# One stay in the 64-row mode per step: moving the 64-row products of a fused FNet and MLP kernel

## Chip, core and metric

The kernel runs on one core of one Trainium2 chip. The metric is the device time of one execution in microseconds (us). Engine names are those of the profile: PE is TensorE's matmul, PEld its weight load, DVE is VectorE, ACT is ScalarE, POOL is GpSimd, SP is SyncE with the DMA queue. L290 is line 290 of the kernel.

## What is computed

The input x has 2048 tokens of 576 features. With xn the layer norm of x over the features, the result is

```
out = x + Re(DFT_seq(DFT_hidden(xn))) + relu(xn @ w1) @ w2
```

w1 is 576 x 4608 and w2 is 4608 x 576; the DFT matrices are inputs, and the real part is `Cr @ a - Ci @ b` of two hidden transforms a and b. Everything is float32 outside.

## The kernel before

**Number format.** Every float32 operand is scaled by a power of two and split into two float16 parts, a high one (index 0) and a low one (index 1). A product is then the sum of three float16 matmuls, high by high, high by low and low by high, accumulated in one PSUM bank. The 576 features are 4 blocks of 128 and a rest of 64.

**The first matrix of the MLP.** The hidden columns are worked through in 9 blocks b of 512 (FB), each in 4 f tiles i of 128 columns (NF). The tokens are worked through in 4 groups g of 512 (G). A step is one pair (b, g), 36 in all. For one f tile, `mlp1` opens a PSUM bank of the pool `ps1` (4 banks) and `mlp1_group` (L288 to L293) runs products of 128 x 512: the 12 of the four whole feature blocks, and one more, `(KM, 0, KM)`, which holds the rest twice over its 128 rows (high part of x in rows 0 to 63, low part in rows 64 to 127, against the high part of w1). What is still missing is the high part of x's rest against the low part of w1's rest, and that has only 64 rows. `mlp1_rest` (L300 to L306) runs it for a pair of f tiles with two 64-row products: the even f tile's on rows 0 to 63 and the odd one's on rows 64 to 127. For that, slot NKX of `xT` holds the high rest a second time in rows 64 to 127. Each of the two closes its f tile's bank.

**After a pair of f tiles**, `mlp1_out` (L308) reads the two banks: ACT L315 and L318 and DVE L319 to L323 form relu, its split and the sums that a seven-product (Strassen-Winograd) block multiplication needs, ACT L325 and DVE L326 split those sums. L323 is the last to read the odd bank, L320 among DVE's the last to read the high half of the even one.

**The second matrix.** `mlp2` (L330) runs one of the seven products q: 12 matmuls of 128 x 288 (L340) into a bank pair of the pool `ps2` (2 pairs), and DVE L346 adds the result to the accumulator.

**The order of a step** is written out in the loop at L642 to L679. The first matrix of step n runs beside the second matrix of step n-1: f tile 0, then q = 0 and 1; f tile 1, the 64-row pair, `mlp1_out` of pair 0, q = 2 and 3; f tile 2, then q = 4 and 5; f tile 3, the 64-row pair, `mlp1_out` of pair 1, q = 6. In between, `work()` takes pieces of the preparation of the next block's weights, and `passes` take the maxima of the sequence-DFT matrices. Steps 0 and 1 and half of step 2 (n == 2, with two f tiles made early) are written out ahead of the loop with other calls.

**What sets the order on an engine.** The framework's planner issues the instructions of each engine mostly in the order of the text; where by its own cost estimate an operand or a buffer isn't ready, it takes the next instruction that is. In the trace PE keeps the text's order in the steps from about 150 us on, and leaves it in the stretch before.

After the steps come the hidden DFT (L709) and the sequence DFT (L810), which the change doesn't touch.

Of the kernel before, what the change touches and what calls it, by code (L numbers as in the profile page):

```python
# [9 lines left out]
F32 = mybir.dt.float32  # L10
# [7 lines left out]
P = 128  # L18
# [6 lines left out]
NF = FB // P  # L25
NQ = NF // 2
G = 512
# [3 lines left out]
KT = 5  # L31
KM = 4
REM = D - KM * P
EH = D // 2
NKX = 2 * KM + 1
# [6 lines left out]
def kernel(  # L42
# [17 lines left out]
    nc = tc.nc  # L60
# [10 lines left out]
    ps1 = tc.alloc_tile_pool(name="ps1", bufs=4, space=PSUM)  # L71
# [96 lines left out]
    xT = [xpool[g].tile([P, NKX + 1, G], F16, name=f"xT{g}") for g in range(NG)]  # L168
# [6 lines left out]
    def stats(ts):  # L175

        n = len(ts)
        mv = small.tile([P, n, 2], F32, tag=f"mv{n}", name=f"mv{ts[0]}")
        sts = [small.tile([P, 2, 6], F32, tag="st", name=f"st{t}", bufs=4) for t in ts]
        for t, st in zip(ts, sts):  # L180
            for j in range(2):
                nc.vector.bn_stats(st[:, j, :], acc[t][:, j * EH : (j + 1) * EH])
                yield
        for i, st in enumerate(sts):
            nc.vector.bn_aggr(mv[:, i], st.rearrange("p a b -> p (a b)"))
            yield
        r0, u, r, sh = (
            small.tile([P, n], F32, tag=f"{a}{n}", name=f"{a}_{ts[0]}") for a in ("r0", "u", "r", "sh")
        )
        m, v = mv[:, :, 0], mv[:, :, 1]  # L190
        stt = nc.vector.scalar_tensor_tensor
        nc.scalar.activation(u, v, AF.Sqrt, bias=eps)
        nc.vector.reciprocal(r0, u)
        yield

        stt(u, v, EPS, r0, ALU.add, ALU.mult)
        yield
        nc.vector.tensor_tensor(u, u, r0, ALU.mult)
        yield
        nc.vector.tensor_scalar(u, u, -0.5 * SX, 1.5 * SX, ALU.mult, ALU.add)  # L200
        yield
        nc.vector.tensor_tensor(r, u, r0, ALU.mult)
        yield
        stt(sh, m, -1.0, r, ALU.mult, ALU.mult)
        for i, t in enumerate(ts):
            means[t], factors[t], shifts[t] = mv[:, i, 0:1], r[:, i : i + 1], sh[:, i : i + 1]

    def weave(steps, *others):

        others = list(others)  # L210
        for _ in steps:
            if others:
                others.pop(0)()
        for f in others:
            f()
# [3 lines left out]
    def normalize(t, eng=nc.vector):  # L219
        stage = dpool.tile([P, 5 * EH], F32, tag="d", name=f"xn{t}")  # L220
        xn = xns[t] = stage[:, :D]

        xs = xss[t] = stage[:, D : 2 * D].bitcast(F16)
        eng.tensor_scalar(xn, acc[t], means[t], factors[t], ALU.subtract, ALU.mult)  # L224
        nc.scalar.activation(xs[:, :D], acc[t], AF.Identity, bias=shifts[t], scale=factors[t])
# [56 lines left out]
    WK = [(kx, hl, k) for k in range(KM) for kx, hl in ((k, 1), (k, 0), (KM + 1 + k, 0))]  # L282
# [2 lines left out]
    WK0 = sorted(WK, key=lambda w: w[1])  # L285
    w1s, w2s, us, hs = {}, {}, {}, {}

    def mlp1_group(b, g, i, cols, ps, wk=WK):  # L288
        for n, (kx, hl, k) in enumerate(wk):
            nc.tensor.matmul(  # L290
                ps[:, cols], w1s[b, i // 2][:, hl, i % 2 * KT + k], xT[g][:, kx, cols],
                start=(n == 0), stop=(n == len(WK) - 1),
            )  # L293

    def mlp1(b, g, i, wk=WK):
        ps = ps1.tile([P, G], F32, tag="ps1", name=f"p1_{b}_{g}_{i}")
        mlp1_group(b, g, i, slice(0, G), ps, wk)
        return ps

    def mlp1_rest(b, g, i, *ps):  # L300

        for r, kx in enumerate((KM, NKX)):
            rows = slice(r * REM, (r + 1) * REM)
            nc.tensor.matmul(  # L304
                ps[r], w1s[b, i][rows, 1, r * KT + KM], xT[g][rows, kx], start=False, stop=True
            )  # L306

    def mlp1_out(b, g, i, pa, pb):  # L308

        h = hs[b, g, i] = mlp.tile([P, 2, 7, GH], F16, tag="h", name=f"h{b}_{g}_{i}", bufs=4)  # L310
        st = mlp.tile([P, 5, GH], F32, tag="stage", name=f"s{b}_{g}_{i}")
        stt = nc.vector.scalar_tensor_tensor
        a11, a21, a12, a22 = pa[:, :GH], pa[:, GH:], pb[:, :GH], pb[:, GH:]
        r21, s1, s2, s3, s4 = (st[:, n] for n in range(5))
        nc.scalar.activation(r21, a21, AF.Relu)  # L315
        for q, src in ((slice(A11, A11 + 1), a11), (slice(A12, A22 + 1), pb)):
            hi, lo = (h[:, n, q].rearrange("p a b -> p (a b)") for n in range(2))
            nc.scalar.activation(hi, src, AF.Relu)  # L318
            stt(lo, src, 0.0, hi, ALU.max, ALU.subtract)  # L319
        stt(s3, a11, 0.0, r21, ALU.max, ALU.subtract)  # L320
        stt(s1, a22, 0.0, r21, ALU.max, ALU.add)
        stt(s2, a22, 0.0, s3, ALU.max, ALU.subtract)
        stt(s4, a12, 0.0, s2, ALU.max, ALU.subtract)  # L323
        hi, lo = (h[:, n, S1 : S4 + 1] for n in range(2))
        order["s"] = nc.scalar.activation(hi, st[:, 1:], AF.Copy).ins  # L325
        order["lo"] = nc.vector.tensor_tensor(lo, st[:, 1:], hi, ALU.subtract).ins  # L326
# [121 lines left out]
    def prepare_block(b):  # L448

        wait = [lambda: None] * 2  # L450
        (m0, s0), (m1, s1) = prepare_w1(b, 0), prepare_w1(b, 1)
        return (
            [lambda: (load_w1(b, 0), load_w1(b, 1))] + wait
            + m0 + m1 + s0 + [lambda: load_w2(b, 0)] + s1 + [lambda: load_w2(b, 1)]
            + wait + prepare_w2(b)
        )
# [17 lines left out]
    ps = [ps1.tile([P, G], F32, tag="ps1", name=f"p1_0_0_{i}") for i in range(NF)]  # L474
# [78 lines left out]
    for t in (8, 9, 10, 11):  # L553
        N(t)
        E(t, GP)
    T(8)
    q2 = [mlp1(0, 1, 2)]
    T(9)
    q2.append(mlp1(0, 1, 3))
# [3 lines left out]
    early = [mlp1(0, 2, 0), mlp1(0, 2, 1)]  # L563
# [7 lines left out]
    def work():  # L571
        if todo:
            todo.pop(0)()
# [5 lines left out]
    def load_d(j):  # L579
        load_raw(("d", j), dft[:, :, j * EH : (j + 1) * EH], [P, KT, EH])  # L580

    def power_d(j):
        if j == 0:
            sc["d"], pw["d"], mx["d"] = cell("sd", 4), cell("pd", 4), cell("md", 4)
        m = slice(j, j + 1)
        magnitude(mx["d"][:, m], raws["d", j])
        power(sc["d"][:, m], pw["d"][:, m], mx["d"][:, m])
# [5 lines left out]
    def split_d(j):  # L593
        split(dsp[j][:, 0], dsp[j][:, 1], raws["d", j], sc["d"][:, j : j + 1])
# [47 lines left out]
    for n in range(2, len(steps)):  # L642
        b, g = steps[n]
        pb, pg = steps[n - 1]
        if g == 0 and b:
            if b + 1 < NB:
                todo += prepare_block(b + 1)
            else:
                todo += [lambda: (load_d(0), load_d(1)), lambda: None, new_d, lambda: None]
                for j in range(4):  # L650
                    todo += [lambda j=j: power_d(j), lambda j=j: split_d(j)]
                    if j < 2:
                        todo += [lambda j=j: load_d(j + 2), lambda: None]
                todo += [scales_d]
        if b == 0 and g + 1 < NG:
            with tc.issue_after(order["lo"]):
                weave(stats([(g + 1) * TG + i for i in range(TG)]))
        ps = []
        for i in range(NF):
            ps.append(early.pop(0) if n == 2 and i < 2 else mlp1(b, g, i, WK[:-1]))  # L660
            if i % 2:
                if n > 2 or i > 2:
                    mlp1_rest(b, g, i // 2, *ps[-2:])
                mlp1_out(b, g, i // 2, *ps[-2:])
            if b == 0 and g + 1 < NG:
                t = (g + 1) * TG + i
                normalize(t)
                remainder(t, nc.gpsimd)
                transposes(t)
            if n == 2 and i == 2:  # L670
                todo += prepare_block(1)
            for _ in range(1 if b else 3):
                work()
            for q in range(2 * i, min(2 * i + 2, 7)):
                mlp2(pb, pg, q)
            for _ in range(1 if b else 3):
                work()
            if n > 3 and i % 2 and passes:
                passes.pop(0)()  # L679
# [115 lines left out]
    for n, (p, kh) in enumerate(units):  # L795
# [4 lines left out]
        for i, (q, rq, first, row, col) in enumerate(PRODUCTS):  # L800
# [5 lines left out]
            ps, w = places[PLACE[i]], csp[m]  # L806
            for k in range(HK):
                r = R[kh * HK + k]
                for j, (a, c) in enumerate(((0, 0), (0, 1), (1, 0))):
                    nc.tensor.matmul(  # L810
                        ps, w[:, a, k], r[:, c, rq],
                        start=first and k == 0 and j == 0, stop=k == HK - 1 and j == 2,
# [4 lines left out]
            if kh and i in (2, 4, 5, 6):  # L817
                h, j = ((0, 0), (1, 1), (0, 1), (1, 0))[(2, 4, 5, 6).index(i)]
                rows = slice((p + h * NP) * P, (p + h * NP + 1) * P)
# [56 lines left out]
```

## Time and profile before

| | |
|---|---|
| three runs | median 1299.18 us, 1298.37 to 3428.88 |
| the profiled execution | 1299.04 us, span 1297.3 us |
| granted TensorE clock | 0.997 of full |
| PE busy | 1274.7 us, 98% of the span |
| DVE, ACT busy | 974.5 us (75%), 530.1 us (41%) |
| L290, 128x512 products | 1798 of 380 ns, 413.6 us |
| L340, 128x288 products | 3024 of 286 ns, 395.1 us |
| L304, 64x512 products | 134 of 386 ns, 26.1 us |

Durations of matmuls in the profile overlap: what one costs in a row of them is the distance between starts. The row's busy time is the union of its spans. "issue" as a releaser means that the engine waited for nothing that the profile shows.

### The profile page before, as it was taken

The numbers are of one execution on the slowest core, as the hardware profiler recorded it, in microseconds if no ns is written. First come the engines' busy times: TensorE is split into PE (matmuls) and PEld (weight loads), VectorE is DVE, ScalarE is ACT, GpSimd is POOL, SyncE is SP. The second block draws the span as 40 slices with busy tenths as digits, with TensorE's granted clock in tenths as the row PEclk, the third lists the DMA queues.
The fourth block names the chain that finished last, engine by engine and source line by source line (L and its number), as shares of the span: only waits on it lengthen the run. The fifth ranks groups of instructions, "written<-read, shape, count | busy, mean of one in ns | idle before, by whom it ended". The sixth has DMA issues, their size and how long they took to land.

```text
span 1297.3 us, 21890 instructions
## 1 busy us (share of the span) xinstructions
PE 1274.7 (98%) x9164; PEld 862.5 (66%) x9164; DVE 974.5 (75%) x1671; ACT 530.1 (41%) x794; POOL 33.8 (3%) x60
## 2 busy tenths in 40 slices
PE   8799999999999999999999999999999999999998
PEld 7565555565565655565555656677777777777777
DVE  8878878587596595685875985568678887888875
ACT  4834344343353442433433442234443333333332
POOL 2210000000000000000000000000000000000000
PEclk9999999999999999999999999999999999999999
DMA  6001213122122132131221222230024435243420
GB/s 240 32 11 59 73 48 127 49 85 91 49 90 83 45 99 67 50 126 50 73 103 50 86 88 86 104 136 17 1 70 158 142 115 165 97 147 121 140 84 19
DMA packets 38002, 112.75 MB, mean 87 GB/s; under 512 B 3984, under 2 KB 10640, under 8 KB 37904
## 3 DMA queue, kind: packets, MB, share of 16 engines
q1 hardware_dynamic: 37904, 111.36, 25.4%
q8 instruction: 71, 1.16, 0.4%
q14 instruction: 27, 0.22, 0.1%
HBM read 101.91 MB, written 9.44 MB: 86 GB/s over the span
## 4 chain that ended last, share of the span: by engine, by line
PE 87%; DVE 6%; DMA 2%; ACT 2%; issue 1%; SPq 1%; POOLq 0%; DVEq 0%; ACTq 0%
PE p L290 27%; PE p L340 26%; PE p L810 25%; PE pd L709 7%; PE p L304 2%; DVE acc L346 1%; DMA raw_d<-in_dft_dram 1%; DMA raw_w<-in_w_dram 1%; DVE w2s L165 1%; DVE h L319 0%; DMA f<-in_cre_dram 0%; ACT xT L247 0%; SPq L80 0%; DVE h L326 0%; DVE xn L224 0%
## 5 line engine op out<-in xcount | busy, mean ns | idle before, releaser
L290 PE MATMUL p<-xT,w1s 128*128 128x512 f16 (+1 forms) x2134 | 434.4, 355 | 2.0 <-ACT xT L247 1.7
L340 PE MATMUL p<-w2s,h 128*128 128x288 f16 x3024 | 395.1, 286 | 3.3 <-DVE acc L346 2.2
L340 PEld LDWEIGHTS <-h 128*128 128x128 f16 x3024 | 290.0, 98 | 104.2 <-issue 18.1
L810 PE MATMUL p<-R,cs 128*128 128x288 f16 x2688 | 329.4, 286 | 0.0
L290 PEld LDWEIGHTS <-w1s 128*128 128x128 f16 x2134 | 195.0, 98 | 189.6 <-issue 4.7
L810 PEld LDWEIGHTS <-cs 128*128 128x128 f16 x2688 | 263.0, 98 | 66.3
L346 DVE SCALAR_TENSOR_TENSOR acc<-p,c_ub,acc 128x576 f32<-128x576 f32 x252 | 204.2, 812 | 47.9 <-PE p L340 47.2
L164 ACT ACTIVATE cs<-c,sc_c 128x1024 f16<-128x1024 f32 x112 | 128.6, 1148 | 203.5 <-PE p L810 147.6
L165 DVE SCALAR_TENSOR_TENSOR cs<-c,sc_c,cs 128x1024 f16<-128x1024 f32 x112 | 143.6, 1282 | 50.1 <-ACT cs L164 41.8
L319 DVE SCALAR_TENSOR_TENSOR h<-p,h 128x256 f16<-128x256 f32 (+1 forms) x144 | 78.3, 551 | 120.7 <-ACT h L318 120.7
L325 ACT ACTIVATE h<-s 128x1024 f16<-128x1024 f32 x72 | 76.1, 1057 | 151.0 <-DVE s L323 151.0
L315 ACT ACTIVATE s<-p 128x256 f32<-128x256 f32 x72 | 27.5, 381 | 246.3 <-PE p L304 246.1
L709 PE MATMUL pd<-dsp,xT 128*128 128x288 f16 x896 | 110.2, 286 | 1.1 <-DVE acc L346 0.9
L326 DVE TENSOR_TENSOR h<-s,h 128x1024 f16<-128x1024 f32 x72 | 88.0, 1223 | 29.3 <-ACT h L325 28.9
L709 PEld LDWEIGHTS <-xT 128*128 128x128 f16 x896 | 87.7, 98 | 23.6 <-issue 1.4
L816 DVE SCALAR_TENSOR_TENSOR o<-p,us_c,o 128x288 f32<-128x288 f32 x112 | 57.4, 513 | 20.6 <-PE p L810 20.5
L635 ACT ACTIVATE f<-f 128x1024 f32<-128x1024 f32 x64 | 66.6, 1041 | 3.8 <-DMA f<-in_cre_dram 3.8
L318 ACT ACTIVATE h<-p 128x512 f16<-128x512 f32 (+1 forms) x144 | 62.8, 491 | 0.2 <-PE p L290 0.2
L164 ACT ACTIVATE w2s<-raw_w,c_sw 128x576 f16<-128x576 f32 (+1 forms) x54 | 43.1, 854 | 29.6 <-DVE raw_w L418 20.4
L165 DVE SCALAR_TENSOR_TENSOR w2s<-raw_w,c_sw,w2s 128x576 f16<-128x576 f32 (+1 forms) x54 | 48.1, 910 | 0.0
L164 ACT ACTIVATE w1s<-raw_w,c_sw 128x640 f16<-128x640 f32 x36 | 28.0, 826 | 17.5 <-DVE c_sw L107 17.4
L727 ACT ACTIVATE R<-pd,c_rho 128x288 f16<-128x288 f32 x48 | 23.8, 499 | 22.8 <-DVE T L721 13.1
(102 smaller groups left out, 676.4 us busy)
## 6 DMA issues: line engine op xcount, KB each, us to landing
f<-in_cre_dram SPq DMA_DIRECT2D x32, 512.0 KB, 3.6
f<-in_cim_dram SPq DMA_DIRECT2D x32, 512.0 KB, 3.5
c<-in_cre_dram SPq DMA_DIRECT2D x32, 512.0 KB, 4.3
c<-in_cim_dram SPq DMA_DIRECT2D x32, 512.0 KB, 4.7
raw_w<-in_w_dram SPq DMA_DIRECT2D x17, 640.0 KB, 4.1
raw_w<-in_w_dram SPq DMA_DIRECT2D x18, 576.0 KB, 3.8
acc<-in_x_dram SPq DMA_DIRECT2D x16, 288.0 KB, 6.0
spill<-acc SPq DMA_DIRECT2D x16, 288.0 KB, 2.5
```

What stands on the lines that cost most here:

```text
L164: nc.scalar.activation(hi, src, AF.Copy, scale=s)
L165: nc.vector.scalar_tensor_tensor(lo, src, s, hi, ALU.mult, ALU.subtract)
L290: nc.tensor.matmul(ps[:, cols], w1s[b, i // 2][:, hl, i % 2 * KT + k], xT[g][:, kx, cols], start=(n == 0), stop=(n == len(WK) - 1),)
L318: nc.scalar.activation(hi, src, AF.Relu)
L319: stt(lo, src, 0.0, hi, ALU.max, ALU.subtract)
L325: order["s"] = nc.scalar.activation(hi, st[:, 1:], AF.Copy).ins
L326: order["lo"] = nc.vector.tensor_tensor(lo, st[:, 1:], hi, ALU.subtract).ins
L340: nc.tensor.matmul(ps[:, c], h[:, x, qa, c * P : (c + 1) * P], w[:, y, qb], start=first and i == 0 and j == 0, stop=i == NQ - 1 and j == 2 ...
L346: nc.vector.scalar_tensor_tensor(o, ps, us[b], o, ALU.mult, ALU.add)
L635: nc.scalar.activation(f, f, AF.Abs, scale=2.0**-10, accum_out=sums_c[:, n, q : q + 1])
L709: nc.tensor.matmul(ps[j], xT[g][:, kx, c * P : (c + 1) * P], dsp[j][:, hl, k], start=(n == 0), stop=(n == len(XK) - 1),)
L810: nc.tensor.matmul(ps, w[:, a, k], r[:, c, rq], start=first and k == 0 and j == 0, stop=k == HK - 1 and j == 2, skip_group_check=not first,)
```

## The change

In each step from n = 3 on, all four 64-row products are issued at the head of f tile 1, behind f tile 0's 13 products and behind q = 0 and 1. The one of f tile 0 closes its bank; those of f tiles 1, 2 and 3 open theirs, so that from then on the four banks of `ps1` are held at once. The 13 products of f tiles 1, 2 and 3 then add to their banks and close them. Rows alternate as before: f tiles 0 and 2 on rows 0 to 63, f tiles 1 and 3 on rows 64 to 127. In step n = 2, f tiles 2 and 3 run a 14th product on 128 rows in place of the 64-row pair.

```diff
-    def mlp1_rest(b, g, i, *ps):
-        for r, kx in enumerate((KM, NKX)):
-            rows = slice(r * REM, (r + 1) * REM)
-            nc.tensor.matmul(
-                ps[r], w1s[b, i][rows, 1, r * KT + KM], xT[g][rows, kx], start=False, stop=True
-            )
+    def mlp1_step(b, g, i, ps):
+        if i == 1:
+            for j in range(NF):
+                r, kx = j % 2, (KM, NKX)[j % 2]
+                rows = slice(r * REM, (r + 1) * REM)
+                if j:
+                    ps.append(new_ps1(b, g, j))
+                nc.tensor.matmul(
+                    ps[j], w1s[b, j // 2][rows, 1, r * KT + KM], xT[g][rows, kx],
+                    start=(j > 0), stop=(j == 0),
+                )
+        if i == 0:
+            ps.append(new_ps1(b, g, 0))
+        mlp1_group(b, g, i, slice(0, G), ps[i], WK[:-1], start=(i == 0), stop=(i > 0))
...
         for i in range(NF):
-            ps.append(early.pop(0) if n == 2 and i < 2 else mlp1(b, g, i, WK[:-1]))
+            if n == 2:
+                ps.append(early.pop(0) if early else mlp1(b, g, i))
+            else:
+                mlp1_step(b, g, i, ps)
             if i % 2:
-                if n > 2 or i > 2:
-                    mlp1_rest(b, g, i // 2, *ps[-2:])
-                mlp1_out(b, g, i // 2, *ps[-2:])
+                mlp1_out(b, g, i // 2, *ps[i - 1 : i + 1])
```

`new_ps1` only opens a bank of `ps1`; `mlp1_group` takes `start` and `stop` so that a group can leave its bank open or add to an open one.

More of the change, by code (lines that the diff above doesn't have):

```diff
@@ L286, with mlp1_group @@
     w1s, w2s, us, hs = {}, {}, {}, {}
-    def mlp1_group(b, g, i, cols, ps, wk=WK):
+    def mlp1_group(b, g, i, cols, ps, wk=WK, start=True, stop=True):
         for n, (kx, hl, k) in enumerate(wk):
@@ L291, in mlp1_group, with new_ps1, mlp1 @@
                 ps[:, cols], w1s[b, i // 2][:, hl, i % 2 * KT + k], xT[g][:, kx, cols],
-                start=(n == 0), stop=(n == len(WK) - 1),
+                start=(start and n == 0), stop=(stop and n == len(wk) - 1),
             )
-    def mlp1(b, g, i, wk=WK):
-        ps = ps1.tile([P, G], F32, tag="ps1", name=f"p1_{b}_{g}_{i}")
-        mlp1_group(b, g, i, slice(0, G), ps, wk)
-        return ps
-    def mlp1_rest(b, g, i, *ps):
-        for r, kx in enumerate((KM, NKX)):
-            rows = slice(r * REM, (r + 1) * REM)
-            nc.tensor.matmul(
-                ps[r], w1s[b, i][rows, 1, r * KT + KM], xT[g][rows, kx], start=False, stop=True
-            )
+    def new_ps1(b, g, i):
+        return ps1.tile([P, G], F32, tag="ps1", name=f"p1_{b}_{g}_{i}")
+    def mlp1(b, g, i):
+        ps = new_ps1(b, g, i)
+        mlp1_group(b, g, i, slice(0, G), ps)
+        return ps
+    def mlp1_step(b, g, i, ps):
[12 more added lines that the diff above has]
+        mlp1_group(b, g, i, slice(0, G), ps[i], WK[:-1], start=(i == 0), stop=(i > 0))
     def mlp1_out(b, g, i, pa, pb):
```

## The prediction

> **What bounds the kernel now.** I read the page first, then the engines' busy time by stretch, then PE's timeline. The page's first part and its chain of waits say that PE is the bound and which lines carry it:
>
> ```profile
> PE 1274.7 (98%) x9164; PEld 862.5 (66%) x9164; DVE 974.5 (75%) x1671; ACT 530.1 (41%) x794; POOL 33.8 (3%) x60
> ...
> PE 87%; DVE 6%; DMA 2%; ACT 2%; issue 1%; SPq 1%; POOLq 0%; DVEq 0%; ACTq 0%
> PE p L290 27%; PE p L340 26%; PE p L810 25%; PE pd L709 7%; PE p L304 2%; DVE acc L346 1%; DMA raw_d<-in_dft_dram 1%; DMA raw_w<-in_w_dram 1%; DVE w2s L165 1%; DVE h L319 0%; DMA f<-in_cre_dram 0%; ACT xT L247 0%; SPq L80 0%; DVE h L326 0%; DVE xn L224 0%
> ```
>
> A share of busy time is a mean over stages, so the stage of the change is looked at by itself: three steps one after another (span, then busy us of PE, PEld, DVE, ACT, POOL).
>
> ```profile
> 591.33:613.70 22.37, 22.37 (x141) 13.34 (x140) 12.50 (x21) 6.49 (x12) 0.00 (x0) 1.00 0.15 48
> 613.70:636.07 22.37, 22.37 (x141) 13.34 (x140) 15.67 (x32) 10.69 (x18) 0.37 (x1) 1.00 0.15 48
> 636.07:658.44 22.37, 22.37 (x141) 13.32 (x140) 21.79 (x47) 10.68 (x18) 0.70 (x2) 1.00 0.31 106
> ```
>
> PE has no gap in any of them, and each takes 22.37 us to the hundredth. DVE has room in two and almost none in the third. So what PE is spared in a step shortens the step, as long as DVE keeps up. PE's timeline of one step (start, length, line, count) gives the prices:
>
> ```profile
> 591.65 0.39 PE L304 MATMUL p<-xT,w1s 64*128 64x512 f16 x2
> 591.97 1.65 PE L340 MATMUL p<-w2s,h 128*128 128x288 f16 x12
> 593.46 2.97 PE L290 MATMUL p<-xT,w1s 128*128 128x512 f16 x13
> 596.26 3.10 PE L340 MATMUL p<-w2s,h 128*128 128x288 f16 x24
> 599.20 2.97 PE L290 MATMUL p<-xT,w1s 128*128 128x512 f16 x13
> 602.10 0.39 PE L304 MATMUL p<-xT,w1s 64*128 64x512 f16 x2
> ```
>
> From starts to starts: 13 products of L290 take 2.80 us (593.46 to 596.26), 0.2155 each; 24 of L340 take 2.94 (596.26 to 599.20), 0.1225 each. The stays in the 64-row mode stand out under a finer timeline, where a weight load (PEld) is to be read beside the product that it is for:
>
> ```profile
> 613.71 0.38 PE L290 MATMUL p<-xT,w1s 128*128 128x512 f16 x1
> 614.02 0.10 PEld L304 LDWEIGHTS <-w1s 64*128 64x128 f16 x2 [0.42 <-issue]
> 614.02 0.39 PE L304 MATMUL p<-xT,w1s 64*128 64x512 f16 x2
> ...
> 614.34 0.10 PEld L340 LDWEIGHTS <-h 128*128 128x128 f16 x1 [0.23 <-issue]
> 614.34 0.30 PE L340 MATMUL p<-w2s,h 128*128 128x288 f16 x1
> ...
> 614.48 0.10 PEld L340 LDWEIGHTS <-h 128*128 128x128 f16 x1
> ```
>
> The two 64-row products start together at 614.02, so they run side by side. But they start 0.31 us behind the L290 before them where 0.2155 is the rule, and the L340 behind starts 0.32 us later where 0.2155 would do; the second L340 is 0.14 behind the first in place of 0.1225. The weight loads at both edges are not ahead of time ("issue"). A stay thus costs 0.095 to enter, 0.2155 for the products, 0.105 to leave and 0.01 behind: 0.43 us, of which 0.21 are its two edges.
>
> **The change part by part.**
>
> One stay is removed per step, two edges: -0.21 us. The four products are two pairs; the pairs share rows, so the second can't run beside the first. The stay that is left costs 0.095 + 2 x 0.2155 + 0.105 + 0.01 = 0.64 us, against 2 x 0.43 = 0.857 before: 0.214 us less. All of it is on PE, which the steps above show as the path. The entry is now from an L340; in the one place where before has that, it is the same (0.22 us from 107.60 to 107.82, 0.1225 being the rule). The exit is into an L290; where before has that, it is 0.32 and 0.23 (130.46, 130.78, 131.01), the same again.
>
> What before doesn't show is a second 64-row product on the same rows within a stay. Its distance to the first can't be under the 0.2155 us that 512 columns take on rows that are used in full, since it uses the same rows; that excludes a gain beyond 0.214. At the upper end it pays an edge like the one at the exit, 0.32, and the step gains only 0.11. I take 0.2155, because the nearest row is the run of L290: there the weights of the next product, for the same rows, are loaded while the one before runs (a load at 613.50 beside the product that began at 613.50, the next product at 613.71).
> The Trainium skill's page "TensorEngine Tiling (Array Packing)", Key Properties, says that a change of mode drains the engine and a change of tile within one doesn't. The 0.31 and 0.32 above agree with its first half; no run here shows the second, by which the sum would be the same 0.214.
>
> Steps: 33 (n = 3 to 35) lose a stay. Not all can use it. In n = 3 and 4 (about 107 to 145 us) PE waits for DVE and the planner has mixed the order; and one step at the load of the hidden-DFT matrices (758.69 to 772.86 between stays, 14.17 us where 11.92 is the rule) is held by DVE: PE waits 0.37 and 1.56 us there. That one gives its 0.2 back. I count 31 of 33: 31 x 0.214 = 6.6 us; with 30 it is 6.4, with 33 it is 7.1.
>
> Step n = 2 loses its stay (0.43) and gets two 128-row products (2 x 0.2155 = 0.43): nothing.
>
> The moved products' waits. Products of f tiles 2 and 3 open their banks at the head of f tile 1, so they wait for the reads of the step before, of which L323 is the last. Queued behind them on PE are all the products of f tiles 1 to 3, and q = 2 to 6. In a plain step L323 of pair 1 ends at 618.20 (617.79 + 0.41), 4.2 us behind the pair's close, and the place where the stay will be, the head of f tile 1, is at 621.57: 3.4 us to spare. In the step with DVE at 97% it is 2.2 us, and the tightest is this one, 1.5 us:
>
> ```profile
> 753.89 0.42 DVE L323 SCALAR_TENSOR_TENSOR s<-p,s 128x256 f32<-128x256 f32 x1
> ...
> 755.79 2.97 PE L290 MATMUL p<-xT,w1s 128*128 128x512 f16 x13
> ```
>
> So this wait costs nothing, hidden behind f tile 0 and q = 0 and 1 (5.7 us of PE). It would cost what L323 is late if DVE lost that room. The cover grows a little: the even bank of a pair now closes with its own 13 products, and ACT's L315 (0.38 us) and first L318 (0.38) no longer wait for the odd one, so DVE's reads can begin up to 0.7 us sooner.
>
> Weights and x: the stay needs the second half of w1's block some 6 us sooner than f tile 2 did. Block 1's last w1 split ends at 108.87 and its first step begins past 120; later blocks are split a step and more ahead. No DMA moves, nothing on SP or POOL, and no DVE or ACT instruction is added.
>
> With DVE at 21.79 of a step that becomes 22.16 us, DVE keeps 0.37 us, and its neighbours have 6 to 9 us: I price that at nothing. If it fails, eight steps (one per block) keep 22.37, and 1.7 us of the gain goes.
>
> The sum is -6.6 us on the profiled execution's 1299.04 us (span 1297.3 and 1.7 around it): 1292.4 us. The median of the three runs is 0.14 above the profiled one, which I leave out.
>
> **The rivals.**
>
> *The second pair pays an edge.* Its weight loads might wait for the first pair, whose rows they share. Then a step gains 0.11 us and the time is 1299.04 - 31 x 0.11 = 1295.6. Against it speak the loads of L290 beside running products on the same rows; for it, that no load at any edge of a stay is ahead of its time. The Trainium skill has this as a rule: "TensorE: Matmul & The Clock Gate", Part 3, The mechanism, says that weight loads overlap running matmuls only where the row groups differ. The rows of L290 above do not agree with it. Chance 0.12.
>
> *The planner takes the four apart* (the side of slower). The planner issues what its estimate holds ready. If by it the bank of f tile 2 or 3 is not released at the head of f tile 1, it puts 128-row products first and comes back. Two stays of a pair cost 0.86, the same as before: 1299. A pair and two single stays cost 0.43 x 3 = 1.29, which is +0.43 a step: 1299.04 + 33 x 0.43 = 1313. Four singles would be 1.71: +0.86 a step, 1327. It decides from the point where, in the plan, L323 ends later than q = 1. For it: the banks come free one by one (L320 of pair 1 ends 1.9 us, L323 4.2 us behind the pair's close), and PE's order is mixed before 150 us. Against it: the 1.5 to 3.4 us of room above, and DVE's order in the trace, where L346 of a q stands about where the q really ends, so the plan's times are not far off. Chance 0.06 for unchanged, 0.06 for 1303 to 1313, 0.02 for more.
>
> *DVE takes the bound in its dense steps.* Then eight steps gain nothing: 1294.1. For it, 97%; against it, PE doesn't wait once there now. Chance 0.1.
>
> **How the numbers follow.** The whole gain in 30 to 33 steps, 1292.0 to 1292.6, has a chance of 0.62; with the small shifts of order in the early steps and behind the last step, which I bound by one stall of before either way (1.6 us), its own range is 1290.7 to 1294.2. The dense steps (0.1) fall at its upper edge and the paying second pair (0.12) at 1295.6. These three make 0.84; the range reaches over them, 1290.5 to 1296.5, and leaves out the planner's rival (0.14) and 0.02 for a larger gain. 2% (26 us) is about what a measurement of this kernel can tell from no change. Faster by that would need 0.79 us a step, nearly all that the two stays cost together (0.86): 0.01. Slower by that is only the case of four single stays: 0.02. Within: 0.97.
>
> **What would show it.** In the profile after, the 64-row line should have 132 products in 33 places, four at a time, the third 0.21 us behind the first (rival: 0.32); 0.64 us from the last product ahead of a stay, less its own length, to the first behind; a step of 22.16 us; and PE without a wait at the stay's third and fourth product. L304's idle "issue" of 27.9 us would be about half. The prediction is wrong if the groups of the 64-row line come in ones and twos, if PE waits for DVE L323, or if steps stay at 22.37 with PE idle.

## The result, and the profile after

The changed kernel takes 1295.41 us (median of 19 runs, 1293.05 to 1298.63), before 1299.04 (19 runs, one of them, at 3428.88, far off): ratio 0.9973, 95% interval 0.9965 to 0.998. The profiled execution took 1296.74 us, span 1295.0. The time lies in the stated range, 3.0 us above the predicted one and outside the likeliest case's own range (1290.7 to 1294.2). Line numbers have moved: L315 is the 64-row line (L304 before), L355 mlp2's product (L340), L361 its accumulation (L346), L334 to L338 and L341 are mlp1_out's on DVE (L319 to L323, L326), L330 and L333 its first ones on ACT (L315, L318). L290, L98 and L165 are as before: L98 takes a maximum of raw weights, L165 splits them.

The page: PE has lost 6.8 us of busy time, but the span only 2.3, and the chain now leads through DVE:

```profile
PE 1267.9 (98%) x9164; PEld 861.7 (67%) x9164; DVE 982.5 (76%) x1671; ACT 537.4 (41%) x794; POOL 35.9 (3%) x60
...
PE 69%; DVE 20%; DMA 5%; ACT 3%; issue 2%; SPq 0%; POOL 0%; POOLq 0%; ACTq 0%; DVEq 0%
```

The timeline of PE and PEld around one stay, read from several narrow windows (start, length, line, count):

```profile
283.58 0.29 PE L355 MATMUL p<-w2s,h 128*128 128x288 f16 x1
...
283.79 0.11 PEld L315 LDWEIGHTS <-w1s 64*128 64x128 f16 x4 [0.24 <-issue]
283.80 0.61 PE L315 MATMUL p<-xT,w1s 64*128 64x512 f16 x4
...
284.02 0.38 PE L315 MATMUL p<-xT,w1s 64*128 64x512 f16 x2
...
284.33 0.11 PEld L290 LDWEIGHTS <-w1s 128*128 128x128 f16 x2 [0.42 <-issue]
284.34 0.39 PE L290 MATMUL p<-xT,w1s 128*128 128x512 f16 x1
...
284.56 0.10 PEld L290 LDWEIGHTS <-w1s 128*128 128x128 f16 x1
```

The second pair begins 0.22 us behind the first (283.80, 284.02), the plain distance of 512 columns, and the weights of all four products are loaded within 0.11 us at the entry. Entry (0.22 from the L355 before) and exit (0.32) cost what they cost in the old stays.

Four steps from stay to stay (span, then busy us of PE, PEld, DVE, ACT, POOL, then the granted TensorE clock, the DMA share and GB/s):

```profile
239.49:261.64 22.15, 22.15 (x141) 13.33 (x141) 12.78 (x21) 7.84 (x14) 0.00 (x0) 1.00 0.15 50
261.64:283.80 22.16, 22.16 (x142) 13.34 (x142) 19.66 (x42) 12.53 (x20) 0.37 (x1) 1.00 0.14 44
283.80:307.35 23.55, 22.48 (x143) 13.32 (x142) 20.52 (x40) 9.57 (x16) 1.19 (x2) 1.00 0.44 135
307.35:329.50 22.15, 22.15 (x141) 13.34 (x141) 12.78 (x21) 6.70 (x12) 0.00 (x0) 1.00 0.20 70
```

Plain steps take 22.157 us, 0.213 less than the 22.370 of before. Once in a block a step takes longer, 23.55 us here, and in it DVE isn't full: 20.52 us of 23.55. Laid beside before by the start of q = 0 in each step, the changed kernel is 1.8 us ahead when the regular steps begin (1.0 of that by the first q = 0, where the change isn't in effect yet); 23 plain steps from there on bring 0.213 each, 4.9 us; seven dense ones give back 0.57, 1.18, 0.92, 1.03, 0.39, 0.75 and 1.07, together 5.9. Against plain steps of 22.157 us the seven are 7.4 us too long. Behind the last of these 1.1 comes back, in the step that DVE held anyway (at the loads of the hidden-DFT matrices), and the last steps and what follows add 0.4. That is the 2.3 us of the profiled pair.

What happens in the dense step is on DVE's timeline (the part in brackets is idle time before, and who ended it):

```profile
287.56 0.81 DVE L98 TENSOR_REDUCE c_mf<-raw_w 128x1 f32<-128x640 f32 x1
288.41 0.15 DVE L380 TENSOR_REDUCE c_mw<-c_mf 128x1 f32<-128x2 f32 x1
289.45 0.16 DVE L106 TENSOR_SCALAR half<-top 128x1 f32<-128x1 f32 x1 [0.89 <-POOL top L104]
289.64 0.15 DVE L107 TENSOR_SCALAR c_sw<-half 128x1 int32<-128x1 int32 x1
289.71 0.14 DVE L111 TENSOR_SCALAR c_pw<-half 128x1 int32<-128x1 int32 x1
291.16 0.82 DVE L98 TENSOR_REDUCE c_mf<-raw_w 128x1 f32<-128x640 f32 x1 [1.30 <-DMA raw_w<-in_w_dram]
291.90 0.68 DVE L334 SCALAR_TENSOR_TENSOR h<-p,h 128x512 f16<-128x512 f32 x1
292.50 0.41 DVE L336 SCALAR_TENSOR_TENSOR s<-p,s 128x256 f32<-128x256 f32 x1
292.83 0.41 DVE L337 SCALAR_TENSOR_TENSOR s<-p,s 128x256 f32<-128x256 f32 x1
293.16 0.81 DVE L361 SCALAR_TENSOR_TENSOR acc<-p,c_ub,acc 128x576 f32<-128x576 f32 x1
```

and on PE's:

```profile
290.09 2.97 PE L290 MATMUL p<-xT,w1s 128*128 128x512 f16 x13
294.02 3.10 PE L355 MATMUL p<-w2s,h 128*128 128x288 f16 x24 [0.96 <-DVE acc L361]
296.96 2.97 PE L290 MATMUL p<-xT,w1s 128*128 128x512 f16 x13
300.04 1.14 PE L355 MATMUL p<-w2s,h 128*128 128x288 f16 x8
```

DVE stands still 0.89 us for GpSimd and 1.30 us for the load of the next w1 block, with mlp1_out's odd half (L334) and the accumulation of q = 2 (L361) queued behind, and PE's q = 4, which uses q = 2's bank, waits for that accumulation: with its 13 products of 2.80 us, f tile 2 would have let it start at 292.89, and it starts at 294.02. There is a second, smaller loss: f tile 3 would let q = 6 start at 299.76, and it starts at 300.04, when the accumulation of q = 4 (L361, 299.18 to 299.98) is through. Such a second loss of 0.27 to 0.28 us stands in six of the seven dense steps; the first, 0.33 to 1.28 us, in all of them. Together they make the 7.4 us.

In the same place before, the third maximum stood behind mlp1_out and both accumulations:

```profile
289.43 1.55 DVE L98 TENSOR_REDUCE c_mf<-raw_w 128x1 f32<-128x640 f32 x2
290.89 1.01 DVE L319 SCALAR_TENSOR_TENSOR h<-p,h 128x256 f16<-128x256 f32 x2
...
293.54 0.41 DVE L323 SCALAR_TENSOR_TENSOR s<-p,s 128x256 f32<-128x256 f32 x1
293.87 0.81 DVE L346 SCALAR_TENSOR_TENSOR acc<-p,c_ub,acc 128x576 f32<-128x576 f32 x1
...
294.66 0.81 DVE L98 TENSOR_REDUCE c_mf<-raw_w 128x1 f32<-128x640 f32 x1
```

The load is later too. SP's issues of the changed kernel (first fence) and of before (second):

```profile
282.07 0.33 SPq L90 DMA_DIRECT2D raw_w<-in_w_dram  x1
283.44 0.33 SPq L643 DMA_DIRECT2D f<-in_cim_dram  x1
284.63 0.33 SPq L90 DMA_DIRECT2D raw_w<-in_w_dram  x1
```

```profile
285.31 0.33 SPq L90 DMA_DIRECT2D raw_w<-in_w_dram  x1
285.99 0.33 SPq L628 DMA_DIRECT2D f<-in_cim_dram  x1
289.36 0.33 SPq L90 DMA_DIRECT2D raw_w<-in_w_dram  x1
```

Three loads of 640, 512 and 640 KB now start within 2.6 us, where it was 4.0; from issue to landing w1's loads take 5.4 us in the median (3.8 to 6.5) against 4.0 (3.8 to 4.8). The planner had freed both raw buffers sooner, by running the splits of w2 that read them without an accumulation between.

**Theory 1.** The stay saves what the sum said. The loss comes from a side of the change that has nothing to do with the 64-row mode: the even bank of a pair now closes ahead of the odd one's 13 products, so ACT's L330 and first L333 and DVE's first L334 can run early; the planner re-packs VectorE's queue around them and pulls the next block's w1 maxima ahead of the odd half and the accumulations. Presumably the load has landed by then in its estimate, which no trace shows; on the chip it hasn't. **The rival** is the prediction's own: VectorE's work in the dense step, 21.8 us before, is too much for 22.16 whatever its order. A second question is what makes the load late.

### The profile page after: what moved, and what is told of

It reads as the page before. It is cut to its first block, busy times and chain, and to the rows that moved or that the text cites. A ratio compares the mean times of both kernels' runs of the same rounds, so it can differ in the third digit from the quotient of the medians.

```text
span 1295.0 us, 21873 instructions
## 1 busy us (share of the span) xinstructions
PE 1267.9 (98%) x9164; PEld 861.7 (67%) x9164; DVE 982.5 (76%) x1671; ACT 537.4 (41%) x794; POOL 35.9 (3%) x60
## 4 chain that ended last, share of the span: by engine, by line
PE 69%; DVE 20%; DMA 5%; ACT 3%; issue 2%; SPq 0%; POOL 0%; POOLq 0%; ACTq 0%; DVEq 0%
PE p L826 25%; PE p L290 18%; PE p L355 18%; PE pd L725 7%; DMA raw_w<-in_w_dram 4%; DVE acc L361 4%; DVE w2s L165 3%; DVE h L334 2%; DVE h L341 2%; DVE w1s L165 1%; PE p L315 1%; ACT j L402 1%; DVE c_mf L98 1%; DVE s L338 1%; DVE s L336 1%
## 5 line engine op out<-in xcount | busy, mean ns | idle before, releaser
L290 PE MATMUL p<-xT,w1s 128*128 128x512 f16 (+1 forms) x2136 | 434.6, 355 | 1.9 <-ACT xT L247 1.5
L355 PE MATMUL p<-w2s,h 128*128 128x288 f16 x3024 | 394.4, 286 | 7.1 <-DVE acc L361 6.0
L355 PEld LDWEIGHTS <-h 128*128 128x128 f16 x3024 | 295.2, 98 | 110.2 <-issue 11.3
L290 PEld LDWEIGHTS <-w1s 128*128 128x128 f16 x2136 | 192.4, 98 | 201.3 <-issue 17.8
L361 DVE SCALAR_TENSOR_TENSOR acc<-p,c_ub,acc 128x576 f32<-128x576 f32 x252 | 204.3, 812 | 37.6 <-PE p L355 35.8
L165 DVE SCALAR_TENSOR_TENSOR cs<-c,sc_c,cs 128x1024 f16<-128x1024 f32 x112 | 143.6, 1282 | 50.8 <-ACT cs L164 42.4
L334 DVE SCALAR_TENSOR_TENSOR h<-p,h 128x256 f16<-128x256 f32 (+1 forms) x144 | 79.6, 554 | 100.9 <-ACT h L333 100.6
L340 ACT ACTIVATE h<-s 128x1024 f16<-128x1024 f32 x72 | 76.1, 1057 | 157.6 <-DVE s L338 157.6
L333 ACT ACTIVATE h<-p 128x512 f16<-128x512 f32 (+1 forms) x144 | 69.6, 485 | 156.5 <-PE p L290 154.4
L341 DVE TENSOR_TENSOR h<-s,h 128x1024 f16<-128x1024 f32 x72 | 88.0, 1222 | 27.5 <-ACT h L340 27.4
L330 ACT ACTIVATE s<-p 128x256 f32<-128x256 f32 x72 | 27.3, 379 | 72.5 <-PE p L315 59.4
L165 DVE SCALAR_TENSOR_TENSOR w2s<-raw_w,c_sw,w2s 128x576 f16<-128x576 f32 (+1 forms) x54 | 48.2, 911 | 7.6 <-ACT w2s L164 7.6
L98 DVE TENSOR_REDUCE c_mf<-raw_w 128x1 f32<-128x640 f32 x36 | 29.1, 812 | 8.1 <-DMA raw_w<-in_w_dram 8.1
```

What stands on the lines that cost most here:

```text
L165: nc.vector.scalar_tensor_tensor(lo, src, s, hi, ALU.mult, ALU.subtract)
L290: nc.tensor.matmul(ps[:, cols], w1s[b, i // 2][:, hl, i % 2 * KT + k], xT[g][:, kx, cols], start=(start and n == 0), stop=(stop and n == l ...
L355: nc.tensor.matmul(ps[:, c], h[:, x, qa, c * P : (c + 1) * P], w[:, y, qb], start=first and i == 0 and j == 0, stop=i == NQ - 1 and j == 2 ...
L361: nc.vector.scalar_tensor_tensor(o, ps, us[b], o, ALU.mult, ALU.add)
```

## The experiments

Each ratio is to the runs of the kernel before on the same chip.

**One stay, banks closed together.** The stay goes behind f tile 1's products, and f tile 2's last product goes behind f tile 3, so each pair's banks close together as in the kernel before.

```diff
...
+        mlp1_group(b, g, i, slice(0, G), ps[i], WK[: 12 if i == 2 else 13], start=(i < 2), stop=(i == 3))
+        if i == 3:
+            mlp1_group(b, g, 2, slice(0, G), ps[2], WK[12:13], start=False)
         if i == 1:
             for j in range(NF):
...
-                    start=(j > 0), stop=(j == 0),
+                    start=(j > 1), stop=(j < 2),
```

> One stay of four 64-row products per step, put behind f tile 1's 13 products, and f tile 2's last product held back behind f tile 3, so that the two banks of each pair close at the same place as before. VectorE's order in the dense step is then again that of before. Theory 1 (the gain of 0.213 us per step is whole, and the early close of the even bank lets the planner put the maxima of the next w1 block ahead of mlp1_out's and mlp2's reads, where VectorE then waits for the load and for GpSimd): every step 22.157 us, the dense ones too, PE waits for L346's counterpart under 2 us in the steps; 33 x 0.213 = 7.0 below before, about 1292. Rival (VectorE's work of 21.8 us in the dense step is the bound, whatever its order): dense steps stay 0.4 to 1.2 us longer than 22.157 and the time is that of the change, about 1295.4.

Measured: 1292.66 us, ratio 0.9953 (0.9939 to 0.9966). All steps from 150 us up to the loads of the hidden-DFT matrices gain 0.213, dense ones too; VectorE has no wait for a w1 load, and PE none for VectorE up to 730 us. The step at those loads loses 0.9 here. Around the dense step, a stretch as long as a step is full on both engines:

```profile
274.00:296.16 22.16, 22.16 (x141) 13.34 (x140) 22.16 (x43) 9.37 (x16) 0.35 (x1) 1.00 0.28 98
```

DVE has no idle time in it at all, and PE hasn't either. Theory 1 holds; the rival, by which DVE's work is too much whatever its order, doesn't.

**The stay behind f tile 1 alone.** As above, without holding f tile 2's last product back; the edit is against the run above.

```diff
-        mlp1_group(b, g, i, slice(0, G), ps[i], WK[: 12 if i == 2 else 13], start=(i < 2), stop=(i == 3))
-        if i == 3:
-            mlp1_group(b, g, 2, slice(0, G), ps[2], WK[12:13], start=False)
+        mlp1_group(b, g, i, slice(0, G), ps[i], WK[:-1], start=(i < 2), stop=(i > 1))
```

> The stay of four behind f tile 1's products in place of ahead of them: pair 0's banks close together again, pair 1's even bank still closes early. VectorE's order is that of before up to the third maximum of w1, and differs behind it. Theory 1: the wait of VectorE for the late load at the third maximum is gone, some wait for GpSimd may stay in the second half of the dense step: 1291.5 to 1293.5. Rival (VectorE's work is the bound): 1295.4.

Measured: 1291.28 us, just below the range, ratio 0.9947 (0.9934 to 0.9959). So it is the early close of pair 0 that does the harm: pair 1's even bank still closes early here, and that costs nothing. A plain step and the dense one:

```profile
263.74:285.90 22.16, 22.16 (x142) 13.34 (x142) 19.74 (x42) 12.53 (x20) 0.37 (x1) 1.00 0.15 49
285.90:308.06 22.16, 22.16 (x143) 13.32 (x142) 20.06 (x39) 9.58 (x16) 1.19 (x2) 1.00 0.45 160
```

PE is full in both. In the place where the changed kernel spent 23.55 us with DVE busy for 20.52, it spends 22.16 with 20.06: nearly the same work, in another order.

**Two stays, banks closed early.** The kernel before, with each pair's stay at the head of its odd f tile (step n = 2 as in the change): the change's VectorE order without its gain.

```diff
...
+        if i % 2:
+            for r, kx in enumerate((KM, NKX)):
+                rows = slice(r * REM, (r + 1) * REM)
+                nc.tensor.matmul(
+                    ps[i - 1 + r], w1s[b, i // 2][rows, 1, r * KT + KM], xT[g][rows, kx],
+                    start=(r == 1), stop=(r == 0),
+                )
+        mlp1_group(b, g, i, slice(0, G), ps[i], WK[:-1], start=(i % 2 == 0), stop=(i % 2 == 1))
```

> The kernel before, two stays of two products per step, but each pair's stay at the head of its odd f tile, so that the even bank closes early as in the change. VectorE's order in the dense step is that of the change; the stays cost what they cost before. Theory 1: the loss alone, 0.4 to 1.2 us in 7 dense steps: 3 to 6 us above before, 1302 to 1305. Rival (a step of 22.16 us is too short for VectorE's work): steps are 22.37 here, so nothing is lost: 1299.

Measured: 1299.29 us, ratio 1.0011 (1.0002 to 1.002): slower by 0.9 us between the medians and by 1.4 by the ratio, where I expected 3 to 6. The time alone fits the rival's 1299 as well, so what the run shows, it shows by its trace, which is one execution (1300.85 us). Five of the seven dense steps in it lose 0.66, 0.23, 3.79, 0.20 and 0.70 us, two lose nothing; 2.25 come back in the step that DVE holds anyway, and 1.5 lie ahead of the regular steps and behind the last. VectorE's waits for w1 loads are there, 6.7 us in 6 places, and in all five steps PE waits for an accumulation (L349). Behind the longest wait for a load, 2.64 us, PE waits 1.96. But not all of the 3.79 is waiting. PE's row, and the same stretch by engines:

```profile
476.05 4.77 PE L343 MATMUL p<-w2s,h 128*128 128x288 f16 x24 [1.96 <-DVE acc L349]
...
476.05:480.75 4.70, 4.70 (x24) 2.99 (x23) 4.46 (x8) 2.10 (x3) 0.84 (x1) 0.64 0.24 81
```

The 24 products took 4.70 us, where 2.94 is the rule, at a granted clock of 0.64. None of the other profiled executions has a lowered clock between 150 and 840 us, so some 1.7 us of this trace say nothing of the order. The other 3.9 do: in this execution the early close loses time in steps of 22.37 us too, which the rival excludes. Why it is less than in the changed kernel wasn't tested; how late each load is, and 0.21 us more room per step, would both fit.

**The passes on even f tiles.** Meant to move the 512 KB loads away from w1's second load.

```diff
-            if n > 3 and i % 2 and passes:
+            if n > 3 and i % 2 == 0 and passes:
```

> The change, with the loads and maxima of the sequence-DFT matrices (512 KB each) moved from the odd to the even f tiles, away from the second load of w1. VectorE's order in the dense step stays that of the change. Theory 1 with the load as cause: that load lands in about 4 us in place of 5.4 to 6.5, VectorE's wait for it (0.9 to 1.4 us) shrinks or goes, the wait for GpSimd (0.55) stays: 1292 to 1294. If the load's lateness is not what matters, 1295.4.

Measured: 1295.97 us, ratio 0.9981 (0.9972 to 0.9989), VectorE's waits for w1 loads 7.1 us in 6 places. Inconclusive: the load of the sequence matrix did not move. It waits for ScalarE's sum on the same buffer, and was issued 1.19 us ahead of w1's second load as before the edit:

```profile
283.33 0.33 SPq L90 DMA_DIRECT2D raw_w<-in_w_dram  x1
284.70 0.33 SPq L643 DMA_DIRECT2D f<-in_cim_dram  x1
285.89 0.33 SPq L90 DMA_DIRECT2D raw_w<-in_w_dram  x1
```

**Without the loads of the sequence matrices.** The kernel leaves out 63 of the 64 loads and sums the first block each time.

```diff
...
-        f = firsts[m] = mlp.tile([P, HK, P], F32, tag="first", name=f"f{n}_{q}", bufs=1)
-        nc.sync.dma_start(f, blocks_c(n)[q])
+        if m == 0:
+            firsts[m] = mlp.tile([P, HK, P], F32, tag="first", name="f0_0", bufs=1)
+            nc.sync.dma_start(firsts[m], blocks_c(n)[q])
...
```

> The change, leaving out 63 of the 64 loads of 512 KB for the maxima of the sequence-DFT matrices: the sums are all of the first block, the same ScalarE work on the same tile. What is left to land in the dense step are the two w1 loads alone. Theory 1 with shared bandwidth as the cause of the late landing: the second w1 load lands in 4 to 4.5 us in place of 5.4 to 6.5, VectorE's wait at the third maximum shrinks by about 1 us and the time falls to 1292 to 1294. If the load is late for another reason (its issue), the wait stays and so does 1295.

Measured: 1288.68 us, ratio 0.9926 (0.9913 to 0.9938). w1's loads land in 3.9 us in the median (3.7 to 5.1), VectorE's waits for them fall from 7.2 us to 2.1, and PE's waits for VectorE between 150 and 730 us, 3.5 in the changed kernel, are gone, though the order still has both halves' maxima ahead of the odd half. So the late landing comes of the 512 KB load between them: each block's second w1 load lands 3.7 to 4.1 us after its issue here and 5.7 to 6.5 in the changed kernel, and the two w1 loads start 2.6 us apart in both. The time came out below what I expected because the step at the hidden-DFT loads gains as well (2.3 us against before).

**The maxima tied.** The change itself, with each later block's w1 maxima queued behind the last VectorE instruction of the mlp1_out ahead of them in the text.

```diff
-        with tc.issue_after(order["lo"]) if b == 1 else nullcontext():
+        with tc.issue_after(order["lo"]) if b else nullcontext():
```

> The change, with VectorE's maxima of every later w1 block tied behind the last VectorE instruction of mlp1_out that the text has before them (as block 1's already are). The planner can then no longer pull them ahead of mlp1_out's odd part and mlp2's reads of the dense step. The stay, and the early close of the even bank, stay as in the change. Theory 1 (the loss is VectorE waiting at those maxima for the w1 load and for GpSimd, with the reads queued behind): VectorE's waits for the load go, all steps 22.157 us but the one at the load of the hidden-DFT matrices, 1291 to 1292. Rival (the early close itself costs, or VectorE's work): 1294 or more.

Measured: 1290.91 us, just below the range, ratio 0.9939 (0.9925 to 0.9952), the lowest ratio of the kernels that compute everything, though its interval overlaps with those of the runs behind f tile 1. The step that took 23.55 us is this one here, from stay to stay, with VectorE's maxima gone to the next:

```profile
282.89:305.04 22.15, 22.15 (x141) 13.34 (x141) 14.22 (x24) 6.70 (x12) 0.00 (x0) 1.00 0.34 113
```

The loads still land late (4.7 us in the median, up to 6.3), and VectorE still waits 6.4 us for GpSimd, but PE waits for VectorE nowhere between 150 and 730 us. The stay and the early close are those of the change, so neither costs anything by itself: the loss hangs on the place of the maxima.

**The tie on the kernel before**, the same edit there, as a control.

> The control: the kernel before with the same tie on the maxima of w1 as in the run of the tied change. Before has no wait of VectorE for those loads (0.2 us in all), so there is nothing to gain: within 0.1% of before, 1297.5 to 1299.5. If the tie is worth several us here too, it is a gain by itself and no cure of the change's loss.

Measured: 1298.62 us, ratio 1.0001 (0.9993 to 1.001). The tie gains nothing that can be told from noise by itself; it cures the change's loss.

**The tie and the stay behind f tile 1.**

> The stay behind f tile 1 and the tie together. Each by itself takes the same loss away, so together they give no more than the stay behind f tile 1 alone: 1290.5 to 1292.

Measured: 1291.49 us, ratio 0.9945 (0.9933 to 0.9958). Two cures of one loss don't add.

What was not tried: a third buffer for raw weights, which would let the load start sooner; no run shows whether SBUF has room for it. Which part of the loss is the wait for GpSimd and which the wait for the load stays open; the tie takes both away.

## Why the prediction was right or wrong

- **PE is the bound, with 0.214 us to gain per step: right.** 22.370 became 22.157 in every plain step, and one stay less is all that PE's timeline shows. (The terms of a stay as the prediction prints them add to a saving of 0.21; unrounded they give the 0.214.) One of the signs was off: the idle "issue" at the 64-row line, 27.9 us, was to be about half, and is 8.4. An entry from a 288-column product shows 0.24 us there, where that from a 512-column one showed 0.42, though both cost the same 0.1.
- **The second pair at 0.2155: right**, 0.22 measured. The rival in which it pays an edge would have given 1295.6, and the median came out at 1295.41; the agreement is chance, since the trace has the distance and it is not 0.32. The Trainium skill's "TensorEngine Tiling (Array Packing)", Key Properties, which says that a change of tile within a mode doesn't drain, agrees with the 0.22. The Trainium skill's "TensorE: Matmul & The Clock Gate", Part 3, The mechanism, by which weight loads overlap running products only on other rows, does not: four loads lie within 0.11 us, two of them for rows on which a product had just begun.
- **The wait for the banks costs nothing: right.** PE has no wait at L315 in the whole trace.
- **The planner takes the four apart: right that it is rare.** It happened in one step, n = 4, which ran three and then one; the other 32 stays have all four.
- **31 of 33 steps can use the gain: wrong**, and this is the step that failed. I said that DVE's dense steps keep 0.37 us, and priced that at nothing; the rival for it, DVE as the bound, I sized at 0.21 us in eight steps, 1.7 us. What came, counted in the same way, is 7.4 us: seven steps missed their 0.213 and were 0.39 to 1.18 us longer than before on top of it (5.9). And the mechanism was not DVE's work: with another order of the same work those steps take 22.16 us (the stay behind f tile 1), even where DVE is busy without a gap (banks closed together). I had seen that the even bank closes early and booked it as 0.7 us of cover; I did not ask what the planner would put into the room that this opens on VectorE, nor what those instructions wait for. The trace of before had a hint: the w1 maxima stood in VectorE's order just behind the accumulations, with 0.2 us of waiting in all.
- **Early steps and the end: near.** The changed kernel was 1.8 us ahead at 150 us, of which 1.0 is scatter from ahead of the change; the rest of it, and the 0.4 at the end, are inside the 1.6 us that I allowed either way. The step at the hidden-DFT loads, which was to give its 0.2 us back, gained 1.1.
- **That the time lies in the stated range is luck.** The range reached up to 1296.5 for a second pair that pays its edge, and none does. The 7.4 us that the dense steps lost were made up in part by 3.3 that the sum didn't have: 1.8 ahead of the regular steps, 1.1 at the hidden-DFT loads, 0.4 at the end.
- **Weights sooner: right.** PE's only wait for w1s is 0.2 us, once.

With the loss taken away, the sum is borne out to about 1 us: 1290.9 to 1292.7 in four kernels with one stay, against 1292.0 to 1292.6 for the whole gain. The 2% that the prediction calls the grain of a measurement is too coarse: the intervals here reach 0.08 to 0.14% to either side.

## What to carry to other kernels

When an instruction is moved, ask not only what waits for it, but what it releases earlier, and what a planner will put into the room on the engine behind it: in VectorE's queue, 97% full in the dense step, an instruction that waits for a load held up all that stood behind it. Tie work that waits for a transfer behind the work that the bound engine needs; here one such line brought the changed kernel from a ratio of 0.9973 to 0.9939. And a stay in the 64-row mode is paid by its edges: a pair alone (0.43 us) costs as much as two full products (2 x 0.2155), so by these prices it pays only where more than one pair share it (0.64 for two).

## What the runs showed of the hardware

- Products on the two 64-row halves start together at the timeline's grain of 0.01 us, and a second pair on the same rows follows in 0.22 us with its weights loaded in advance. Entering the mode costs about 0.1 us, the same behind 288-column products (0.22 less 0.1225) and 512-column ones (0.31 less 0.2155); so does leaving it (0.32 less 0.2155).
- Loads of 640, 512 and 640 KB issued within 2.6 us stretch the last one's landing to 5.7 to 6.5 us; without the 512 KB one it takes 3.7 to 4.1.
- In one execution the granted TensorE clock fell behind a wait of 1.96 us: 0.64 over the 24 products that followed (4.70 us in place of 2.94). Waits of up to 1.77 us in the steps of the other traces had no such sequel. Whether the wait caused it stays open.
